# A list scheduler gets other weights: attention with a gated mixture on one Trainium2 core

## The chip, the core and the metric

The kernel runs on one core of a Trainium2 chip. The metric is the device time of one execution in microseconds (us); for the kernel before, three executions took 1042.3, 1046.54 and 1048.9 us, median 1046.54. TensorE (PE) multiplies matrices into PSUM, VectorE (DVE), ScalarE (ACT) and GpSimd (POOL) work on tiles, and SyncE (SP) issues all the transfers here: loads, stores, and transfers that transpose on the way.

## The reference

```python
kv_pool = kv.reshape(B, H // r, r, W // r, r, C).mean(axis=(2, 4))    # r = 4
k = v = kv_pool.reshape(B, -1, C) @ w_sr                              # 768 keys of 128
s = scale * (q @ k.transpose(0, 2, 1)); s = s - s.max(-1, keepdims=True)
a = np.exp(s); a /= a.sum(-1, keepdims=True) + 1e-09
x = a @ v
gate_pre[t] = sum over the five taps k of conv_w[k] * x[t - 4 + k]
out = (1 / (1 + np.exp(-gate_pre)) * (x @ w_val)) @ w_out
```

There are 4 batches of 12288 queries of 128 channels. All is float32, and the kernel keeps that accuracy by splitting values into a high and a low part.

## The kernel before

The queries are cut into groups of 512 columns, 24 to a batch, counted here from 0 to 95 and on (the last 512 columns make two half groups), and each group into four row blocks of 128, counted 0 to 3. For each row block PE makes one score block (L480: high query by high key, high by low, low by high, six matmuls into a PSUM tile `s` of 128 x 768), VectorE takes the row maximum (`nm`, L492), ScalarE the exponential with the row sum (L499), VectorE the reciprocal (`r`, L508 and L513), ScalarE writes the high half of the normalised row as fp16 (`hl`, L527), and VectorE the low half (`hl`, L538, called `lo` below). That last one is the last reader of the score tile. There are three such tiles, so a score waits until the `lo` of the score three places ahead of it is done.

Two row blocks at a time go from `hl` to `pt` by a transposing transfer (L551), two transfers to a group: the first for row blocks 0 and 1, the second for 2 and 3. When both are there, PE adds up 18 attention-value products (L622) into `av`; ScalarE copies that to `x` (L640); GpSimd makes five taps and four sums of the gate (L679, L687); ScalarE takes its tanh (L698); PE makes the value product (L702), VectorE multiplies (`h`, L706), PE makes the output product (L711, into the one PSUM tile `m`, as L702 does), ScalarE copies it out (`o`, L716), and every second group a store goes (L739).

The keys and values of a batch are made ahead, while the batch before is worked on: 16 loads (`kvt`, L279), each summed by VectorE in two parts (`pool`, L291), then projections (L314, L400). Queries are loaded for two groups at a time (L452).

Each engine executes its instructions in the order in which the program issues them. That order is made before anything runs, by a list scheduler (the class `Plan`). Every step is entered with its engine, a duration, a due time (a shift from the table `DUE`, measured from the group's time `t0`, the group's number times `PERIOD`), the steps it waits for and the buffers that it takes and gives back. `order()` then goes through a model of time: of the engine whose next step can begin first, it takes, of the steps that can begin within `WAIT` of it, the one with the earliest due time; on SP, a copy that follows a copy has its due time lowered by `CLUMP`. A step's result is there after its duration and a lag, a transfer's after a lead, its duration and a tail. Nothing of this model is in the program that runs; only the order is. Transfers of both kinds are issued on the one SP queue, in order. In the model the second transposition of a group also waits for the first one's end, since the first takes the `pt` tile (`owner`); the transfers write different halves of it.

Of the kernel before, what the change touches and what calls it, by code (L numbers as in the profile page):

```python
# [19 lines left out]
PIECES = 16  # L20
PARTS = 2

PERIOD = 10.09
DUE = dict(keys=-40.9, vals=-34.18, q=-55.15, qh=8.39, ql=-72.29,
           score=(-7.32, -5.54, -6.8, -6.2), max=(-13.84, -0.53, 9.94, -17.87),
           exp=(2.41, -23.38, 0.25, -11.15), hi=(-29.46, -24.26, -5.96, -31.79),
           lo=(12.82, -20.44, -2.27, 2.53), turn=(1.5, 15.54, 23.77, 4.89), pe=7.53, thi=54.02,
           tlo=9.93, r=(-44.99, -41.46, -38.33, -16.57), grid=-1.44, av=20.99, avs=4.41,
           halo=59.69, x=42.03, gate=31.71, th=61.17, val=48.0, h=0.01, out=29.31,
           evac=16.32, store=49.62)  # L30


class Step:
# [8 lines left out]
class Plan:  # L42
# [2 lines left out]

    EDGE = 0.04
    LAG = dict(PE=0.16, ACT=0.1, DVE=0.085, POOL=0.04, SP=0.0)
    WAIT = dict(PE=0.14, ACT=0.41, DVE=0.11, POOL=0.05, SP=0.32)
    DMA_LEAD, DMA_TAIL, CLUMP = 1.3, 0.8, 23.19

    def __init__(self):
        self.steps, self.stock = [], {}
# [14 lines left out]
    def order(self):  # L67
        left, later = {}, {}
        ready = {}
        for s in self.steps:  # L70
            left[s] = len(s.after)
            for a in s.after:
                later.setdefault(a, []).append(s)
            if not left[s]:
                ready.setdefault(s.eng, []).append((s.start, s))
        free = {e: 0.0 for e in ("PE", "ACT", "DVE", "POOL", "SP")}
        last = {e: "" for e in free}
        dma = 0.0
        until, placed = {}, []
        while any(ready.values()):  # L80
            best = None
            for e, items in ready.items():
                ests = []
                for at, s in items:
                    t = max(at, free[e])
                    for name in s.takes:
                        stock = self.stock[name]
                        t = max(t, min(stock)[0]) if stock else 1e18
                    if t < 1e17:
                        ests.append((t, s))  # L90
                if not ests:
                    continue
                t0 = min(t for t, _ in ests)
                s = min((s.due - (s.kind == last[e] == "copy") * self.CLUMP, n, s)
                        for n, (t, s) in enumerate(ests) if t <= t0 + self.WAIT[e])[2]
                t0 = next(t for t, x in ests if x is s)
                if best is None or t0 < best[0]:
                    best = (t0, e, s)
            assert best, "no step can begin"
            t, e, s = best  # L100
            ready[e] = [x for x in ready[e] if x[1] is not s]
            for name in s.takes:
                stock = self.stock[name]
                pick = min(stock)
                stock.remove(pick)
                s.slot[name] = pick[1]
            if e == "SP":
                copy = s.kind == "copy"
                free[e] = t + (0.5 if copy else s.dur)
                switch = 1.0 if last[e] == "copy" and not copy else 0.0  # L110
                dma = max(dma + switch, t + self.DMA_LEAD) + s.dur
                s.end = dma + self.DMA_TAIL
            else:
                free[e] = t + s.dur
                s.end = t + s.dur + s.lag
            last[e] = s.kind
            placed.append(s)
            for owner, name in s.frees:
                owner.users[name] -= 1
                until[owner, name] = max(until.get((owner, name), 0.0), s.end)  # L120
                if not owner.users[name]:
                    self.stock[name].append((until[owner, name] + self.EDGE, owner.slot[name]))
            for n in later.get(s, ()):
                left[n] -= 1
                if not left[n]:
                    at = max([n.start] + [a.end + self.EDGE for a in n.after])
                    ready.setdefault(n.eng, []).append((at, n))
        assert len(placed) == len(self.steps), "steps that wait for each other"
        return placed
# [13 lines left out]
def cost(us, n):  # L143

    return 0.06 + (us - 0.06) * n / NT
# [3 lines left out]
def attn_moe_kernel(ctx, tc, qT, kvT, w_sr, w_moe, outT):  # L149
# [12 lines left out]
    HALO = TAPS - 1  # L162
    T = PERIOD
    D = DUE
# [3 lines left out]
    plan = Plan()  # L168
# [267 lines left out]
    def group(g, prev, nxt):  # L436
        st, n, w = g.st, g.n, g.n * P
        t0 = g.at * T
# [6 lines left out]
        ld = g.io.ld  # L445
        if off == 0 or g.i == 1:
            cols = GQ if g.i < 2 else 2 * GQ

            def load():
                if off == 0:  # L450
# [4 lines left out]
            ld = plan.add("SP", 1.6 * cols / (2 * GQ), at, load, [ld],  # L455
                          takes=("q",) if off == 0 else (), start=at)
# [7 lines left out]
        def ql():  # L464
# [1 line left out]
            nc.gpsimd.tensor_tensor(out=g.ql, in0=g.io.q[:, mine], in1=g.qh.bitcast(F32),  # L466
                                    op=ALU.subtract)

        s_qh = plan.add("ACT", cost(0.51, n), t0 + D["qh"], qh, [ld], takes=("qh",))
        s_ql = plan.add("POOL", cost(1.23, n), t0 + D["ql"], ql, [s_qh], takes=("ql",),  # L470
                        frees=[(g.io.ld, "q")])
        g.hls, g.los, g.ready = {}, {}, []
# [46 lines left out]
        def straight(j, sc, r):  # L519
# [4 lines left out]
            def hi():  # L524
                if own:
# [4 lines left out]
                            takes=("hl",) if own else ())  # L530
# [5 lines left out]
            def lo():  # L536
# [1 line left out]
                v.scalar_tensor_tensor(out=hl[:, half, 1], in0=sc.tile[:, :NK], scalar=r.tile,  # L538
                                       in1=hl[:, half, 0], op0=ALU.mult, op1=ALU.subtract)
            s_lo = plan.add("DVE", 0.925, t0 + j * T / 4 + D["lo"][j], lo, [s_hi],  # L540
                            frees=[(sc, "s"), (r, "r")])
            g.los[j] = s_lo
            alone = not half and j + 1 in g.turned
            if not (half or alone):
# [1 line left out]
            width, j0 = (1, j) if alone else (2, j - 1)  # L546

            def turn():
                if g.pt_by is s_t:
# [1 line left out]
                nc.sync.dma_start_transpose(  # L551
                    out=g.pt[:, j0:j0 + width].rearrange("p j k q -> p (j k) q"),
                    in_=g.hls[j // 2][:, :width].rearrange("p j a k -> p (j a k)"))
            s_t = plan.add("SP", 1.4 * width, t0 + j * T / 4 + D["turn"][j], turn,
                           [s_lo] if alone else [s_lo, g.los[j - 1]],
                           takes=() if g.pt_by else ("pt",),
                           frees=[(g.hl_by, "hl")], kind="turn")
# [49 lines left out]
        for j in range(n):  # L607
            sc = score(j)
            mx = row_max(j, sc)
            r = unit_over_z(j, sc, expo(j, sc, mx))  # L610
# [6 lines left out]
        avs = []  # L617
        for i, (name, k, a) in enumerate(AV):
# [5 lines left out]
            frees = [(g.pt_by, "pt")] if i == len(AV) - 1 else []  # L624
# [14 lines left out]
        def x():  # L639
# [6 lines left out]
                          start=t0)  # L646
        g.s_halo = s_halo
        g.s_x = plan.add("ACT", cost(0.49, n), t0 + D["x"], x, [avs[-1], s_halo],
                         frees=[(avs[0], "av")])


        late = t0 + D["gate"]
# [19 lines left out]
        else:  # L672
# [12 lines left out]
            def plus(k, tap, before):  # L685
                def run():
                    nc.gpsimd.tensor_tensor(out=g.gate, in0=g.gate, in1=tap.tile, op=ALU.add)  # L687
                return plan.add("POOL", cost(1.24, n), late, run, [tap, before],
                                frees=[(tap, f"tap{k}")])

            gate = gate_by = pool_tap(0)
# [21 lines left out]
        def evac():  # L713
            if off == 0:
# [5 lines left out]
        s_val = plan.add("PE", 0.215 * n, t0 + D["val"], val, [g.s_x, st["wb_by"]]  # L720
                         + ([] if tail else [s_th]), takes=("m",), frees=held)
        s_h = plan.add("DVE", cost(0.59, n), t0 + D["h"], h, [s_val, s_th], takes=("h",),
                       frees=[(s_val, "m"), (s_th, "th")])
        s_out = plan.add("PE", 0.215 * n, t0 + D["out"], out, [s_h], takes=("m",),
                         frees=[(s_h, "h")])
        s_ev = plan.add("ACT", cost(0.48, n), t0 + D["evac"], evac,
# [69 lines left out]
```

## Time and profile before

| what | value |
|---|---|
| three executions | 1042.3, 1046.54, 1048.9 us |
| the profiled execution | 1041.52 us |
| its span, first to last instruction | 1039.7 us |
| mean granted TensorE clock | 0.993 |
| PE, DVE, ACT, POOL busy | 95%, 91%, 85%, 88% of the span |
| transfers | 227 MB, 218 GB/s |

The profile is of one execution. Busy times of PE are modelled at their ends, since matmuls overlap: a busy PE may still have waited for parts of a microsecond. The chain of waits goes back from the last instruction, at each step to what released it.

### The profile page before, as it was taken

How to read it: one execution, taken by the hardware profiler on the slowest of the kernel's cores; microseconds unless marked ns; L12 is line 12 of the kernel's file. 1: busy time of each engine (PE TensorE's matmuls, PEld its weight loads, DVE VectorE, ACT ScalarE, POOL GpSimd, SP SyncE). 2: the span in 40 equal slices, each digit the busy share in tenths (PEclk: the TensorE clock that was granted, in tenths of full speed). 3: DMA queues.
4: the chain of work that ended last, by engine and by line, in shares of the span. 5: the costliest groups of instructions: out<-in, count | busy, mean ns of one | idle time of the engine just before them, and what ended most of it. 6: DMA issues, size and time to landing. Idle time of an engine off the chain costs nothing.

```text
span 1039.7 us, 15330 instructions
## 1 busy us (share of the span) xinstructions
PE 989.9 (95%) x4514; PEld 599.2 (58%) x4514; DVE 941.8 (91%) x1830; ACT 878.7 (85%) x1567; POOL 919.8 (88%) x1047
## 2 busy tenths in 40 slices
PE   1699999999999999999999999999999999999997
PEld 0455555556665555556665555555656666665653
DVE  6889999989899999899989999999998898988985
ACT  1678888889888888789898888888989999999883
POOL 1159989989999999889999999999999999999994
PEclk9899999999999999999999999999999999999999
DMA  8599999999999999999999999999999999999982
GB/s 315 131 200 233 240 244 231 247 233 197 195 241 243 233 242 245 231 234 198 208 219 243 238 237 245 228 251 230 193 202 225 209 199 221 204 209 198 184 177 83
DMA packets 616707, 227.06 MB, mean 218 GB/s; under 512 B 595504, under 2 KB 595888, under 8 KB 616624
## 3 DMA queue, kind: packets, MB, share of 16 engines
q1 hardware_dynamic: 616624, 226.07, 100.3%
q8 instruction: 37, 0.61, 0.2%
q14 instruction: 46, 0.38, 0.1%
HBM read 50.66 MB, written 25.17 MB: 73 GB/s over the span
## 4 chain that ended last, share of the span: by engine, by line
PE 79%; DVE 11%; DMA 7%; ACT 1%; issue 1%; SPq 0%; ACTq 0%; DVEq 0%
PE s L480 33%; PE av L622 30%; PE m L711 8%; PE m L702 7%; DMA pt<-hl 5%; DVE hl L538 4%; DVE nm L492 4%; DMA kvt<-in_kv 2%; DVE pool L291 2%; DVE h L706 1%; ACT hl L527 1%; DVE r L513 0%; PE m L314 0%; DVE wb L375 0%; PE s L314 0%
## 5 line engine op out<-in xcount | busy, mean ns | idle before, releaser
L687 POOL TENSOR_TENSOR gate<-gate,tap 128x512 f32<-128x512 f32 x376 | 481.6, 1281 | 9.8
L538 DVE SCALAR_TENSOR_TENSOR hl<-s,r,hl 128x768 f16<-128x768 f32 x382 | 386.8, 1013 | 49.1 <-ACT hl L527 48.7
L622 PE MATMUL av<-pt,vh 128*128 128x512 f16 (+1 forms) x1164 | 377.9, 379 | 5.0 <-DMA pt<-hl 4.9
L499 ACT ACTIVATE s<-s,nm 128x768 f32<-128x768 f32 x384 | 336.4, 876 | 43.7 <-DVE nm L492 43.1
L527 ACT ACTIVATE hl<-s,r 128x768 f16<-128x768 f32 x382 | 339.0, 906 | 39.1 <-DVE r L513 21.9
L492 DVE TENSOR_REDUCE nm<-s 128x1 f32<-128x768 f32 x384 | 362.7, 945 | 8.7 <-PE s L480 8.0
L480 PE MATMUL s<-kh,qh 128*128 128x512 f32 (+1 forms) x768 | 267.9, 430 | 13.5 <-DVE hl L538 7.7
L679 POOL TENSOR_SCALAR tap<-x,wb 128x512 f32<-128x512 f32 x376 | 253.5, 693 | 0.0
L622 PE MATMUL av<-pt,vl 128*128 128x512 f16 (+1 forms) x582 | 219.7, 378 | 0.0
L480 PEld LDWEIGHTS s<-kh,qh 128*128 128x128 f32 x768 | 133.8, 191 | 132.4 <-issue 59.2
L480 PE MATMUL s<-kl,qh 128*128 128x512 f32 (+1 forms) x768 | 199.1, 341 | 0.0
L480 PE MATMUL s<-kh,ql 128*128 128x512 f32 (+1 forms) x768 | 198.0, 339 | 0.0
L622 PEld LDWEIGHTS <-vh 128*128 128x128 f16 x1164 | 108.5, 98 | 153.1 <-issue 60.8
L466 POOL TENSOR_TENSOR ql<-q,qh 128x512 fp32r<-128x512 f32 (+1 forms) x97 | 122.6, 1264 | 48.8 <-ACT qh L462 48.2
L480 PEld LDWEIGHTS s<-kl,qh 128*128 128x128 f32 x768 | 119.2, 191 | 17.6 <-DVE kl L348 0.5
L480 PEld LDWEIGHTS s<-kh,ql 128*128 128x128 f32 x768 | 119.0, 190 | 17.2
L711 PE MATMUL m<-h,wm 128*128 128x512 f32 (+1 forms) x194 | 102.5, 610 | 2.0 <-DVE h L706 1.9
L702 PE MATMUL m<-x,wb 128*128 128x512 f32 (+1 forms) x194 | 98.5, 589 | 1.2 <-ACT o L716 1.2
L622 PEld LDWEIGHTS <-vl 128*128 128x128 f16 x582 | 57.2, 98 | 66.5 <-issue 23.4
L679 POOL TENSOR_SCALAR gate<-x,wb 128x512 f32<-128x512 f32 x94 | 65.1, 693 | 33.7 <-ACT x L640 26.6
L716 ACT ACTIVATE o<-m 128x512 f32<-128x512 f32 (+1 forms) x97 | 57.6, 593 | 37.9 <-PE m L711 36.7
L513 DVE RECIPROCAL r<-r 128x1 f32<-128x1 f32 x384 | 62.9, 164 | 13.1
(56 smaller groups left out, 592.2 us busy)
## 6 DMA issues: line engine op xcount, KB each, us to landing
kvt<-in_kv SPq DMA_DIRECT2D x64, 384.0 KB, 4.2
q<-in_q SPq DMA_DIRECT2D x47, 512.0 KB, 4.4
out<-o SPq DMA_DIRECT2D x47, 512.0 KB, 3.9
pt<-hl SPq DMA_TRANSPOSE x191, 6.0
q<-in_q SPq DMA_DIRECT2D x2, 256.0 KB, 5.6
raw<-in_w_moe SPq DMA_DIRECT2D x1, 261.0 KB, 5.3
out<-o SPq DMA_DIRECT2D x1, 256.0 KB, 2.0
out<-o SPq DMA_DIRECT2D x2, 128.0 KB, 1.7
```

The costliest lines, as they stand in the source:

```text
L466: nc.gpsimd.tensor_tensor(out=g.ql, in0=g.io.q[:, mine], in1=g.qh.bitcast(F32), op=ALU.subtract)
L480: nc.tensor.matmul(t[:, c0:c1], a[:, sl], k[:, c0:c1], start=(i == 0), stop=(i == 2))
L492: v.tensor_reduce(out=s.tile, in_=sc.tile[:, :NK], axis=AX.X, op=ALU.max, negate=True)
L499: nc.scalar.activation(out=sc.tile[:, :NK], in_=sc.tile[:, :NK], func=AF.Exp, bias=mx.tile, accum_out=sc.tile[:, NK:NK + 1])
L513: v.reciprocal(out=s.tile, in_=e.tile)
L527: nc.scalar.activation(out=g.hls[j // 2][:, half, 0], in_=sc.tile[:, :NK], func=AF.Copy, scale=r.tile)
L538: v.scalar_tensor_tensor(out=hl[:, half, 1], in0=sc.tile[:, :NK], scalar=r.tile, in1=hl[:, half, 0], op0=ALU.mult, op1=ALU.subtract)
L622: nc.tensor.matmul(g.av, st[name][:, k * P:(k + 1) * P], g.pt[:, :, a * NCH + k], start=(i == 0), stop=(i == len(AV) - 1))
L679: nc.gpsimd.tensor_scalar(out=s.tile, in0=src(k), scalar1=wt(k), scalar2=1.0, op0=ALU.mult, op1=ALU.mult)
L687: nc.gpsimd.tensor_tensor(out=g.gate, in0=g.gate, in1=tap.tile, op=ALU.add)
L702: nc.tensor.matmul(g.m, st["wb"][:, :C], g.x[:, HALO:], start=True, stop=True)
L711: nc.tensor.matmul(g.m2, wout, g.h, start=True, stop=True)
```

## The change

`PERIOD`, all of `DUE`, `WAIT` and the transfer figures of the model get other numbers; some durations and lags of single steps too; and the model's SP queue is held longer by a transposition (until `TURN_TAIL` before its end, or 1.05 of its duration, whichever is later, where it was its duration). The steps, their buffers and what they wait for stay.

```diff
-PERIOD = 10.09
-DUE = dict(keys=-40.9, vals=-34.18, q=-55.15, qh=8.39, ql=-72.29,
-           score=(-7.32, -5.54, -6.8, -6.2), max=(-13.84, -0.53, 9.94, -17.87),
...
+PERIOD = 10.07
+DUE = dict(keys=-51.54, vals=-33.1, q=-59.95, qh=11.92, ql=-52.61,
+           score=(-9.11, -6.7, -6.23, -7.04), max=(-11.45, 1.22, 7.36, -15.65),
...
-    WAIT = dict(PE=0.14, ACT=0.41, DVE=0.11, POOL=0.05, SP=0.32)
-    DMA_LEAD, DMA_TAIL, CLUMP = 1.3, 0.8, 23.19
+    WAIT = dict(PE=0.13, ACT=0.31, DVE=0.12, POOL=0.01, SP=0.7)
+    DMA_LEAD, DMA_TAIL, TURN_TAIL, CLUMP = 1.5, 0.9, 1.7, 25.3
...
-                free[e] = t + (0.5 if copy else s.dur)
                 switch = 1.0 if last[e] == "copy" and not copy else 0.0
                 dma = max(dma + switch, t + self.DMA_LEAD) + s.dur
                 s.end = dma + self.DMA_TAIL
+                free[e] = t + 0.5 if copy else max(t + 1.05 * s.dur, s.end - self.TURN_TAIL)
...
-            s_t = plan.add("SP", 1.4 * width, t0 + j * T / 4 + D["turn"][j], turn,
+            s_t = plan.add("SP", 1.45 * width, t0 + j * T / 4 + D["turn"][j], turn,
```

What the order becomes is shown at three places, all around groups 27 to 32, where the keys of batch 2 are loaded during batch 1. The first is the SP queue. Names are buffer and tile number; two rows with the same `pt` are the two transpositions of one group. Before, from the first transposition of group 28 to the second of group 29:

```order
L551 DMA_TRANSPOSE pt0_3677<-hl0_3584 128x24x128
L279 DMA kvt0_3725<-in_kv 128x768
L279 DMA kvt1_3737<-in_kv 128x768
L551 DMA_TRANSPOSE pt0_3677<-hl1_3661 128x24x128
L551 DMA_TRANSPOSE pt1_3785<-hl2_3735 128x24x128
L452 DMA q1_3813<-in_q 128x1024
L739 DMA out_0<-o0_3746 128x1024
L551 DMA_TRANSPOSE pt1_3785<-hl3_3787 128x24x128
```

After, from the first transposition of group 27 (`pt3_3574`) to the second of group 29:

```order
L551 DMA_TRANSPOSE pt3_3574<-hl1_3472 128x24x128
L551 DMA_TRANSPOSE pt0_3687<-hl0_3598 128x24x128
L551 DMA_TRANSPOSE pt3_3574<-hl3_3549 128x24x128
L551 DMA_TRANSPOSE pt0_3687<-hl2_3667 128x24x128
L551 DMA_TRANSPOSE pt1_3807<-hl1_3734 128x24x128
L279 DMA kvt2_3844<-in_kv 128x768
L279 DMA kvt3_3855<-in_kv 128x768
L452 DMA q1_3861<-in_q 128x1024
L739 DMA out_0<-o0_3729 128x1024
L551 DMA_TRANSPOSE pt1_3807<-hl0_3785 128x24x128
```

The four copies of two groups now stand in one run instead of two, and the first transposition of group 28 stands ahead of the second of group 27. Over the whole program such a pair of groups comes 14 times in the new order and never in the old. In the stretches without loads a copy stood behind the two transpositions of a group, and now stands between them.

The second place is PE, between score 1 of group 29 and score 0 of group 30, which takes its buffer. Before, the first rows behind score 1 of group 29 (six more attention products and score 3 follow ahead of score 0 of group 30):

```order
L702 MATMUL m0_3701<-x0_2831,wb1_2823 128x512
L480 MATMUL s2_3707<-kh1_2631,qh2_3436 128x512
L480 MATMUL s2_3707<-kh1_2631,qh2_3436 128x256
L480 MATMUL s2_3707<-kl1_2652,qh2_3436 128x512
L480 MATMUL s2_3707<-kl1_2652,qh2_3436 128x256
L480 MATMUL s2_3707<-kh1_2631,ql2_3450 128x512
L480 MATMUL s2_3707<-kh1_2631,ql2_3450 128x256
L622 LDWEIGHTS vh1_2787
L622 MATMUL av0_3721<-pt3_3541,vh1_2787 128x512
L711 MATMUL m0_3727<-h0_3716,wm_69 128x512
L622 LDWEIGHTS vl1_2802
L622 MATMUL av0_3721<-pt3_3541,vl1_2802 128x512
```

After, from behind score 1 of group 29 (the rest of score 3 and then at once score 0 of group 30 follow):

```order
L711 MATMUL m0_3710<-h0_3704,wm_69 128x512
L480 MATMUL s2_3720<-kh1_2251,qh2_3409 128x512
L480 MATMUL s2_3720<-kh1_2251,qh2_3409 128x256
L480 MATMUL s2_3720<-kl1_2265,qh2_3409 128x512
L480 MATMUL s2_3720<-kl1_2265,qh2_3409 128x256
L480 MATMUL s2_3720<-kh1_2251,ql2_3434 128x512
L480 MATMUL s2_3720<-kh1_2251,ql2_3434 128x256
L702 MATMUL m0_3737<-x2_3522,wb1_2705 128x512
L711 MATMUL m0_3753<-h1_3746,wm_69 128x512
L480 MATMUL s0_3765<-kh1_2251,qh2_3409 128x512
L480 MATMUL s0_3765<-kh1_2251,qh2_3409 128x256
L480 MATMUL s0_3765<-kl1_2265,qh2_3409 128x512
```

The attention products of group 27 have moved behind score 0 of group 30, all 18 in one run, and an L711 stands directly behind its own L702. In the whole program PE changes 241 times from attention products to a score before, and 233 times after.

The third place is VectorE, where a load's sum (`pool`) stands. Before, the first load behind the first transposition of group 30 (`kvt2_3977`) is summed behind the maximum of score 3 of group 31 (`nm1_4031`):

```order
L538 SCALAR_TENSOR_TENSOR hl2_3983<-s2_3916,r9_3975,hl2_3983 128x768
L538 SCALAR_TENSOR_TENSOR hl2_3983<-s0_3937,r0_3996,hl2_3983 128x768
L508 SCALAR_TENSOR_TENSOR r11_4017<-s1_3955,unit_61 128x1
L513 RECIPROCAL r2_4028<-r11_4017 128x1
L492 TENSOR_REDUCE nm1_4031<-s2_4009 128x1
L291 TENSOR_REDUCE pool0_3300<-kvt2_3977 128x24
```

After, the first load behind the first transposition of group 29 (`kvt2_3844`) is summed behind the maximum of score 3 of group 30 (`nm3_3891`):

```order
L492 TENSOR_REDUCE nm3_3891<-s1_3871 128x1
L508 SCALAR_TENSOR_TENSOR r4_3899<-s0_3846,unit_61 128x1
L513 RECIPROCAL r6_3902<-r4_3899 128x1
L291 TENSOR_REDUCE pool0_3054<-kvt2_3844 128x24
L538 SCALAR_TENSOR_TENSOR hl3_3829<-s2_3833,r3_3889,hl3_3829 128x768
L538 SCALAR_TENSOR_TENSOR hl2_3906<-s0_3846,r6_3902,hl2_3906 128x768
```

In both, one group lies between the transposition ahead of the load and the sum; in the new order that transposition itself stands behind four others in a row.

## Rows read from the trace of the kernel before

**Rows 1.** The page: busy time of each engine (share of the span), and the transfers' rate in 40 slices of the span.

```profile
PE 989.9 (95%) x4514; PEld 599.2 (58%) x4514; DVE 941.8 (91%) x1830; ACT 878.7 (85%) x1567; POOL 919.8 (88%) x1047
...
GB/s 315 131 200 233 240 244 231 247 233 197 195 241 243 233 242 245 231 234 198 208 219 243 238 237 245 228 251 230 193 202 225 209 199 221 204 209 198 184 177 83
```

**Rows 2.** Busy time by stretch, four stretches cut where the batches turn over: stretch, its length, then busy us (and instructions) of PE, PE's weight loads, DVE, ACT and POOL, granted clock, share and rate of the transfers. The last stretch, and the sum of all four.

```profile
756.20:1005.90 249.70, 249.63 (x1153) 152.40 (x1152) 222.78 (x426) 223.63 (x398) 240.08 (x272) 1.00 0.99 205
sum 925.40, PE 915.39 PEld 554.17 DVE 855.37 ACT 818.60 POOL 876.67; mean PE 228.85 PEld 138.54 DVE 213.84 ACT 204.65 POOL 219.17
```

**Rows 3.** The chain of waits between 300 and 345 us, two groups of a stretch with loads: start, length, what.

```profile
319.37 0.86 PE m L702 x2
320.23 1.05 PE s L480 x6
...
325.11 2.61 PE av L622 x12
...
339.60 0.86 PE m L702 x2
```

**Rows 4.** The timeline between 900 and 925 us, a stretch without loads: start, length, engine, line and operation. The end of a score, the value product of one group and of the next, the score that takes the buffer, and the first attention product of a group.

```profile
905.53 0.51 PE L480 MATMUL s<-kh,ql 128*128 128x512 f32 x2
...
905.87 1.02 PE L702 MATMUL m<-x,wb 128*128 128x512 f32 x2
...
911.49 0.59 PE L480 MATMUL s<-kh,qh 128*128 128x512 f32 x2
...
915.85 1.02 PE L702 MATMUL m<-x,wb 128*128 128x512 f32 x2
...
918.68 0.38 PE L622 MATMUL av<-pt,vh 128*128 128x512 f16 x1
```

**Rows 5.** The timeline of the SP queue between 326 and 350 us (loads): start, how long the issue holds the queue, what.

```profile
323.25 8.49 SPq L551 DMA_TRANSPOSE pt<-hl  x2
331.79 1.05 SPq L279 DMA_DIRECT2D kvt<-in_kv  x2
332.94 8.90 SPq L551 DMA_TRANSPOSE pt<-hl  x2
341.93 0.53 SPq L452 DMA_DIRECT2D q<-in_q  x1
343.03 0.34 SPq L739 DMA_DIRECT2D out<-o  x1
343.47 8.78 SPq L551 DMA_TRANSPOSE pt<-hl  x2
```

**Rows 6.** The same of the SP queue between 906 and 920 us (no loads).

```profile
906.00 3.59 SPq L551 DMA_TRANSPOSE pt<-hl  x1
909.69 0.53 SPq L452 DMA_DIRECT2D q<-in_q  x1
911.41 8.13 SPq L551 DMA_TRANSPOSE pt<-hl  x2
```

**Rows 7.** The timeline between 329 and 338 us: the way of one score block, from its last matmuls over maximum, high half and low half to the next score in its buffer.

```profile
330.00 0.52 PE L480 MATMUL s<-kh,ql 128*128 128x512 f32 x2
...
330.72 0.95 DVE L492 TENSOR_REDUCE nm<-s 128x1 f32<-128x768 f32 x1
...
334.04 0.89 ACT L527 ACTIVATE hl<-s,r 128x768 f16<-128x768 f32 x1
...
334.97 1.02 DVE L538 SCALAR_TENSOR_TENSOR hl<-s,r,hl 128x768 f16<-128x768 f32 x1 [0.34 <-ACT hl L527]
...
336.13 0.59 PE L480 MATMUL s<-kh,qh 128*128 128x512 f32 x2
```

**Rows 8.** Who waited for whom, PE: us in total, times, longest.

```profile
PE av L622 <- DMA pt<-hl: 4.9, 7, 0.9
```

**Rows 9.** The transpositions (how long an issue holds the queue, in ns, min/median/max), their landing after the issue, one late landing from the chain of waits, and the landing of the loads behind the start.

```profile
L551 SPq DMA_TRANSPOSE pt<-hl x191: 2880/3717/6558, 34.7 to 1011.4; - x191
...
DMA to landing us min/median/max: 4.6/6.0/9.3
...
137.31 9.03 DMA pt<-hl
...
DMA to landing us min/median/max: 3.4/3.9/6.3
```

**Rows 10.** Around 420 us: from the chain of waits the value products ahead and behind and a load; from the timeline VectorE's sum of that load and the next score, with the idle time before each and what ended it in brackets; and the stretch from 424.5 to 427 us with the granted clock (the third figure from the end).

```profile
411.26 0.86 PE m L702 x2
...
414.52 5.87 DMA kvt<-in_kv
...
435.26 0.86 PE m L702 x2
...
420.42 0.55 DVE L291 TENSOR_REDUCE pool<-kvt 128x24 f32<-128x384 f32 x1 [2.31 <-DMA kvt<-in_kv]
...
423.16 0.59 PE L480 MATMUL s<-kh,qh 128*128 128x512 f32 x2 [1.93 <-DVE r L508]
...
424.50:427.00 2.50, 2.50 (x5) 1.37 (x6) 2.50 (x3) 1.43 (x4) 2.00 (x4) 0.50 1.17 239
```

**Rows 11.** The timeline of PE at the end of the program, where an L711 follows its own L702.

```profile
1028.41 1.10 PE L702 MATMUL m<-x,wb 128*128 128x512 f32 x2
1030.37 1.12 PE L711 MATMUL m<-h,wm 128*128 128x512 f32 x2 [0.86 <-DVE h L706]
```

More of the change, by code (lines that the diff above doesn't have):

```diff
@@ L21 @@
 PARTS = 2
-PERIOD = 10.09
-DUE = dict(keys=-40.9, vals=-34.18, q=-55.15, qh=8.39, ql=-72.29,
-           score=(-7.32, -5.54, -6.8, -6.2), max=(-13.84, -0.53, 9.94, -17.87),
[L26 to L30, printed above, removed]
+PERIOD = 10.07
+DUE = dict(keys=-51.54, vals=-33.1, q=-59.95, qh=11.92, ql=-52.61,
+           score=(-9.11, -6.7, -6.23, -7.04), max=(-11.45, 1.22, 7.36, -15.65),
+           exp=(-10.02, -18.03, 5.52, -8.91), hi=(-20.54, -25.94, -10.8, -36.78),
+           lo=(8.83, -56.87, -0.25, -1.79), turn=(24.53, 12.45, 5.45, 5.14), pe=9.87, thi=27.66,
+           tlo=31.15, r=(-39.49, -44.12, -34.32, -11.39), grid=0.16, av=20.26, avs=5.48,
+           halo=77.01, x=41.77, gate=27.88, th=54.09, val=46.93, h=-7.7, out=14.11, evac=-6.98,
+           store=58.22)
 class Step:
@@ L467, in ql @@
                                     op=ALU.subtract)
-        s_qh = plan.add("ACT", cost(0.51, n), t0 + D["qh"], qh, [ld], takes=("qh",))
+        s_qh = plan.add("ACT", cost(0.51, n), t0 + D["qh"], qh, [ld], takes=("qh",), lag=0.145)
         s_ql = plan.add("POOL", cost(1.23, n), t0 + D["ql"], ql, [s_qh], takes=("ql",),
@@ L540, in straight @@
             s_lo = plan.add("DVE", 0.925, t0 + j * T / 4 + D["lo"][j], lo, [s_hi],
-                            frees=[(sc, "s"), (r, "r")])
+                            frees=[(sc, "s"), (r, "r")], lag=0.19)
             g.los[j] = s_lo
@@ L648, in group @@
         g.s_x = plan.add("ACT", cost(0.49, n), t0 + D["x"], x, [avs[-1], s_halo],
-                         frees=[(avs[0], "av")])
+                         frees=[(avs[0], "av")], lag=0.17)
         late = t0 + D["gate"]
@@ L687, in run @@
                     nc.gpsimd.tensor_tensor(out=g.gate, in0=g.gate, in1=tap.tile, op=ALU.add)
-                return plan.add("POOL", cost(1.24, n), late, run, [tap, before],
+                return plan.add("POOL", cost(1.26, n), late, run, [tap, before],
                                 frees=[(tap, f"tap{k}")])
@@ L722, in group @@
         s_h = plan.add("DVE", cost(0.59, n), t0 + D["h"], h, [s_val, s_th], takes=("h",),
-                       frees=[(s_val, "m"), (s_th, "th")])
+                       frees=[(s_val, "m"), (s_th, "th")], lag=0.15)
         s_out = plan.add("PE", 0.215 * n, t0 + D["out"], out, [s_h], takes=("m",),
```

## The prediction, made blind

> **What bounds the kernel now.** I went from the page to the stretches between the batches, then to one period of each kind of stretch, then to the two things that touch there: the SP queue and the score buffers. The page [rows 1] shows TensorE busy for 95% of the span; the other engines follow at 85 to 91%. Cut where the batches turn over [rows 2], TensorE is busy 915 of the 925 us of the body. The last stretch, 756 to 1006 us, has no key/value loads and TensorE busy 249.6 of 249.7 us; there one group takes 9.98 us, from one value product (L702) at 905.87 to the next at 915.85 [rows 4]. Where the next batch's keys are loaded ("load stretch" below), two groups take 20.23 us, from 319.37 to 339.60, against 2 x 9.98 = 19.96 [rows 3].
>
> Two loops explain the difference. In the load stretch the SP queue never rests: from 323.25 to 343.47 us every issue starts within 0.7 us of the end of the one before it, and the round of two loads, one query copy, one store and four transpositions takes 20.2 us, which is the pair's time [rows 5]. In the last stretch the same queue has pauses, as from 910.22 to 911.41 us ahead of a transposition [rows 6]. And TensorE cannot run ahead of the three score buffers: the score block that ends at 330.52 is reduced, exponentiated, normalised and split, its last reader `lo` ends at 335.99, and the score that takes its buffer starts at 336.13, so 5.61 us after the first one ended [rows 7]. In the last stretch the same loop closes in 5.45 us (906.04 to 911.49) [rows 4]. TensorE is the chain, with these two loops close behind it.
>
> **The change, part by part.** No instruction is added or taken away; only order changes. So each part is a place where something comes nearer to, or farther from, what it waits for. I count PE work with rows 3: score block 1.05 us, attention-value product 2.61/12 = 0.22, L702 or L711 0.86.
>
> *Stretches without loads* (groups 70 to 93, and the ends of the other batches): PE's order differs only in two attention products of group g-2 ahead of score 3 of group g instead of three; the buffer loop that closes in 5.45 us contains the same work. A copy now stands between the two transpositions of a group. It puts the later one behind 0.5 us of issue, and even the longest landing, 9.3 us [rows 9], is covered: the one issued at 906.00 [rows 6] is first read at 918.68 [rows 4], 12.7 us later. Zero.
>
> *Queue relief in the load stretch.* Before, loads and query/store copies stand apart, two runs of copies per two groups; now all four copies come in one run, sometimes with six transpositions in a row behind it. Two transpositions behind a run of two copies hold the queue 8.5 to 8.9 us [rows 5], 8.1 behind a single copy [rows 6]: the copies are paid for there too, and fewer runs leave fewer such places. If the relief is complete, TensorE's 19.96 us per pair is the next bound: 0.27 us per pair. Behind the start come 48 loads, two to a pair, so 24 pairs, of which the first four are split up: 20 x 0.27 = -5.4 us. At worst there is no relief, 0; at most all 24, -6.5. I take -5.4, since the queue of rows 5 has nothing but back-to-back issues.
>
> *Scores too near their buffer.* Score 0 of group 30 needs the buffer of score 1 of group 29. Before, PE does L702, a score, eight attention products, L711 and a score in between: 0.86 + 1.05 + 8 x 0.22 + 0.86 + 1.05 = 5.6 us, just the loop. Now it does L711, score, L702, L711, score: 3 x 0.86 + 2 x 1.05 = 4.7 us. It waits 0.75 us against 5.45, 0.9 against 5.61. In groups 8 to 69 there are 16 such places under 5.3 us in the new order, and 3 in the old. Added up in order, each wait pushing what follows, they cost 8.0 us now and 1.3 before against a loop of 5.45, and 11.4 and 3.1 against 5.6: +6.7 to +8.4 us. At the low end 0, if they fall into waits that are there anyway. I take +6.7, because the loop of rows 4 is the undisturbed one.
>
> *L711 directly behind its L702* happens four times in the body (before only in the tail). The tail shows its price: L702 starts at 1028.41, L711 at 1030.37, 1.96 - 0.86 = 1.1 us of waiting for `h` [rows 11]. Three of the four stand just ahead of one of the near scores and spend its wait, so +1 us; 0 to 4.4.
>
> *Transpositions out of order.* Fourteen times the first transposition of group g+1 is issued ahead of the second one of g; before, never. SP is in order, so group g's second one waits until g+1's `lo` is done. For g = 27: from the end of score 1 of group 28, 5.45 us to its `lo`, 3.7 us of queue for its transposition, then 4.6, 6.0 or 9.3 us to the landing of the other [rows 9]: 13.8, 15.2 or 18.5. PE's work over the same way is seven scores (7.4), 18 products (3.9) and four L702/L711 (3.4): 14.7, and the near scores' 0.75 on top: 15.4. So no wait at the median, 3.1 us at the worst landing, 14 x 3.1 = 43 us if all were the worst. Waits of this kind cost 4.9 us in the profile [rows 8], one of them behind a landing of 9.0 us after copies [rows 9]. I take 0: as many remain.
>
> *Loads and their sums.* [...] That pair takes 24.0 us, 411.26 to 435.26, so 3.8 more than 20.2 [rows 10]. Whether it stays is open: -3.8 to +23 (ten places, below). I take 0. The start gains or loses some tenths: +0.5 for nearer scores there.
>
> Sum: -5.4 + 6.7 + 1 + 0 + 0 + 0.5 = **+2.8 us**. The profiled execution took 1041.5 us, so 1044.3; the median of the three runs, 1046.5, stands 5.0 above it, so about **1049 us**.
>
> [...] A transposition of 128 x 3072 fp16 values, 786 KB, holds the queue for 3.7 us [rows 9], 212 GB/s, against 315 GB/s in the first slice of the page [rows 1], which is copies alone. [...]
>
> **The rivals.** *First, the queue frees more than it costs* (faster). The relief is complete, the 4.9 us of late transpositions go with it, the stall at 420 us does not return, and the near scores fall into waits that are no longer visible: -5.4 - 4.9 - 3.8 = -14.1, so 1027.4 and with the 5.0 about 1032 us. For it: all of these rows hang on one saturated queue. Against: sixteen near places do not depend on the queue.
>
> *Second, VectorE runs into loads that have not landed* (slower). The loads now follow transposition 0 of a group that has itself three others ahead of it. For the load summed after the row maximum of score 3 in group 30: from the end of score 1 of group 28, 5.45 us to its `lo`, four transpositions at 3.7, 3.9 us to the load's landing [rows 9]: 24.2 us; PE's way to there is 9.0 to score 1 of group 29, 13.3 to score 3 of group 30, 1.1 for the maximum: 23.4. Short by 0.8 before any wait. In the old order the load stands behind one transposition: 5.45 + 3.7 + 3.9 = 13.1 against 15.6. By sums of this kind ten loads of groups 8 to 69 fall short by some 1 to 3 us, and none did. If each costs what VectorE waited at 420 us, 10 x 2.3 = +23: 1041.5 + 2.8 + 23 + 5 = 1072 us; with half of them, 1061. It decides from a shortfall that TensorE's own waits do not cover, about 1 us. For it: VectorE is in order and every score passes through it twice. Against: the waits of the other terms give the loads time.
>
> *Third, the queue is not what sets the load pace.* Then the relief is 0 and the rest stays: 2.8 + 5.4 = +8.2, 1055 us. Were a transposition worth its bytes at 315 GB/s, 2.5 us, the round would be 4 x 2.5 + 1.84 MB/315 GB/s = 15.8 us, under TensorE's 19.96, and the cause of 20.23 would be elsewhere. The back-to-back issues of rows 5 speak against it. [...]
>
> **How the numbers follow.** Forecast 0.48, first rival 0.22, second 0.20, third 0.10. The forecast is the likeliest case, 1049 us; its own range is 1043 to 1056. The range 1032 to 1066 leaves out half of the first rival and the upper half of the second, 2 in 10 together. One per cent, 10.5 us, is about what a measurement of this kernel can tell from no change. Faster than 1036: 0.18 of the first rival and 0.02 of the forecast, 0.20. Slower than 1057: 0.18 of the second, 0.04 of the third, 0.05 of the forecast, 0.27. Within: 0.53.
>
> **What would show it.** Relief: pairs near 19.96 us in the load stretch and pauses in SP's timeline there. Near scores: TensorE waiting for `hl` of VectorE just ahead of L480, at the 16 places, 0.3 to 1.5 us each. Out-of-order transpositions: more or less than 4.9 us of attention products waiting for `pt`. Loads: VectorE's sums (L291) waiting for `kvt`, now 2.3 us in the body. The last stretch has to stay at 9.98 us per group; if it does not, the argument about order is wrong as a whole.

## The result: 0.7% slower

Seven executions of the changed kernel take 1051.83 to 1054.31 us, median 1052.33; seven of the kernel before, beside them, have a median of 1046.54. The ratio is 1.0067, with a 95% interval of 1.0045 to 1.0088: +5.8 us by the medians. The forecast was 1049 us, its own range 1043 to 1056.

The profiled execution took 1054.31 us, 12.8 more than that of before, which stood 5.0 under its median. Its page, as in [rows 1]:

```profile
PE 994.4 (94%) x4514; PEld 598.5 (57%) x4514; DVE 940.7 (89%) x1830; ACT 879.9 (84%) x1567; POOL 918.3 (87%) x1047
```

Where the time went shows in the busy time by stretch, cut at the value products of groups 17, 41, 65 and 90 in both kernels (columns as in [rows 2]). Before, the two stretches with loads behind the start:

```profile
260.00:508.80 248.80, 245.88 (x1123) 148.53 (x1122) 231.73 (x451) 218.25 (x390) 233.90 (x266) 0.99 1.06 229
508.80:756.20 247.40, 244.53 (x1123) 147.34 (x1122) 231.48 (x451) 218.18 (x390) 233.75 (x265) 1.00 1.06 230
```

After, these two and the last:

```profile
259.10:514.50 255.40, 248.16 (x1122) 147.21 (x1121) 231.89 (x451) 219.09 (x391) 233.30 (x264) 0.99 1.05 224
514.50:768.90 254.40, 245.91 (x1122) 147.18 (x1121) 231.70 (x451) 219.13 (x391) 233.39 (x264) 1.00 1.05 223
768.90:1018.30 249.40, 249.40 (x1152) 152.29 (x1151) 222.58 (x423) 224.50 (x400) 240.58 (x273) 1.00 1.00 204
```

The loss is in the stretches with loads, 6.6 and 7.0 us; the start is 0.9 us shorter, and the last stretch keeps its time [rows 2]. That is more than the 5.8 us of the medians. The stretches compare better than whole executions, because the start varies: a kernel below that keeps the order of before (the short sums) took 6.0 us more than before up to group 17, and then the same 248.7 and 247.5 us. Who waited in the whole program, as in [rows 8], for PE and its weight loads:

```profile
PE av L622 <- DMA pt<-hl: 7.1, 7, 2.1
...
PEld L622 <- DMA pt<-hl: 3.8, 4, 2.2
```

10.9 us of waiting for transpositions, where it was 4.9. The SP queue's timeline shows how a transposition comes to be late, around those of groups 34 and 35:

```profile
397.14 3.72 SPq L551 DMA_TRANSPOSE pt<-hl  x1
...
403.77 3.59 SPq L551 DMA_TRANSPOSE pt<-hl  x1
...
407.42 3.71 SPq L551 DMA_TRANSPOSE pt<-hl  x1
```

and VectorE's low halves (`lo`) around them, with the first attention product of group 34:

```profile
397.13 1.01 DVE L538 SCALAR_TENSOR_TENSOR hl<-s,r,hl 128x768 f16<-128x768 f32 x1
...
402.69 1.02 DVE L538 SCALAR_TENSOR_TENSOR hl<-s,r,hl 128x768 f16<-128x768 f32 x1
...
413.10 0.39 PE L622 MATMUL av<-pt,vh 128*128 128x512 f16 x1
```

The `lo` that ends at 398.14 is the last that group 34's second transposition needs, and the queue is free at 400.86. But the first of group 35 stands ahead, and its `lo` ends at 403.71. So the queue stands still for 2.91 us, then takes that one, and group 34's goes out at 407.42, 6.6 us after it could have. It lands at 413.06, and the product starts 0.04 us later, so it had no slack left; at groups 30 and 48 the products wait 1.91 and 2.06 us. There are eight such pauses of 0.9 to 3.9 us ahead of an out-of-order pair in the two stretches, 16.1 us together. All the queue's pauses over 0.3 us came to 8.5 and 10.6 us before (270 to 500 and 520 to 745 us), and come to 16.6 and 15.8 after.

### The profile page after: what moved, and what is told of

It is laid out like the page before. It is cut to its first block, busy times and chain, and to the rows that moved or that the text cites. A ratio compares the mean times of both kernels' runs of the same rounds, so it can differ in the third digit from the quotient of the medians.

```text
span 1052.5 us, 15285 instructions
## 1 busy us (share of the span) xinstructions
PE 994.4 (94%) x4514; PEld 598.5 (57%) x4514; DVE 940.7 (89%) x1830; ACT 879.9 (84%) x1567; POOL 918.3 (87%) x1047
## 5 line engine op out<-in xcount | busy, mean ns | idle before, releaser
L538 DVE SCALAR_TENSOR_TENSOR hl<-s,r,hl 128x768 f16<-128x768 f32 x382 | 385.3, 1013 | 45.0 <-ACT hl L527 43.2
L622 PE MATMUL av<-pt,vh 128*128 128x512 f16 (+1 forms) x1164 | 367.5, 380 | 7.1 <-DMA pt<-hl 7.1
L480 PE MATMUL s<-kh,qh 128*128 128x512 f32 (+1 forms) x768 | 262.1, 423 | 15.5 <-DVE hl L538 8.5
L622 PE MATMUL av<-pt,vl 128*128 128x512 f16 (+1 forms) x582 | 220.5, 379 | 0.0
L480 PEld LDWEIGHTS s<-kh,qh 128*128 128x128 f32 x768 | 133.0, 191 | 133.4 <-issue 57.4
L480 PE MATMUL s<-kl,qh 128*128 128x512 f32 (+1 forms) x768 | 198.6, 340 | 0.0
L480 PE MATMUL s<-kh,ql 128*128 128x512 f32 (+1 forms) x768 | 198.1, 339 | 0.0
L622 PEld LDWEIGHTS <-vh 128*128 128x128 f16 x1164 | 106.7, 98 | 145.0 <-issue 49.3
L480 PEld LDWEIGHTS s<-kl,qh 128*128 128x128 f32 x768 | 119.0, 190 | 17.9 <-DVE kl L348 0.5
L480 PEld LDWEIGHTS s<-kh,ql 128*128 128x128 f32 x768 | 118.7, 190 | 17.0
L711 PE MATMUL m<-h,wm 128*128 128x512 f32 (+1 forms) x194 | 103.1, 613 | 5.5 <-DVE h L706 5.1
L622 PEld LDWEIGHTS <-vl 128*128 128x128 f16 x582 | 57.2, 98 | 76.9 <-issue 27.3
L702 PE MATMUL m<-x,wb 128*128 128x512 f32 (+1 forms) x194 | 98.5, 589 | 1.2 <-ACT o L716 1.2
L706 DVE SCALAR_TENSOR_TENSOR h<-th,m 128x512 f32<-128x512 f32 (+1 forms) x97 | 65.4, 674 | 10.4 <-PE m L702 10.0
```

The source lines that it names most:

```text
L480: nc.tensor.matmul(t[:, c0:c1], a[:, sl], k[:, c0:c1], start=(i == 0), stop=(i == 2))
L622: nc.tensor.matmul(g.av, st[name][:, k * P:(k + 1) * P], g.pt[:, :, a * NCH + k], start=(i == 0), stop=(i == len(AV) - 1))
L702: nc.tensor.matmul(g.m, st["wb"][:, :C], g.x[:, HALO:], start=True, stop=True)
L706: v.scalar_tensor_tensor(out=g.h, in0=g.th, scalar=1.0, in1=g.m, op0=ALU.add, op1=ALU.mult)
L711: nc.tensor.matmul(g.m2, wout, g.h, start=True, stop=True)
```

## The experiments

Theory Q says that these pauses make the loss. Theory N is my prediction's: the scores too near their buffer. To change one thing at a time, most kernels let the scheduler make its order, edit the finished list of one engine, and issue the steps by these lists; what isn't edited keeps its place. The times are medians, and the ratios are to the kernel before on the same chip (medians of 1044.0 to 1045.9 us there).

**Transpositions in order.** On the list of SP:

```diff
+def in_order(sp):
+    for i in range(len(sp) - 1):
+        a, b = sp[i].name, sp[i + 1].name
+        if a and b and a[0] == b[0] == "T" and a[1] == b[1] + 1:
+            sp[i], sp[i + 1] = sp[i + 1], sp[i]
```

> The changed kernel with one edit of its finished order: on the SP queue, the 14 transpositions that stand ahead of the second one of the group before change places with it; every other engine keeps its order. Theory Q (the queue's head waits for scores not yet made, while a transposition that is ready stands behind it): the eight pauses of 0.9 to 3.9 us read there in the trace, 16 us of queue time, go, and half of it or more reaches the end: 1041 to 1046 us, against 1052.3 of the changed kernel. Theory N (the scores that stand too near their buffer make the loss, as I predicted): 1051 to 1053.

1045.62 us, ratio 1.0004 (0.9987 to 1.0020): by the times, the loss is gone. The waits of PE and of its weight loads:

```profile
PEld L645 <- DMA pt<-hl: 1.1, 1, 1.1
...
PE av L645 <- DMA pt<-hl: 0.8, 1, 0.8
```

1.9 us instead of 10.9. Group 34's second transposition now goes out as soon as the first has left the queue, the second of these rows:

```profile
396.48 3.16 SPq L573 DMA_TRANSPOSE pt<-hl  x1
...
399.73 3.75 SPq L573 DMA_TRANSPOSE pt<-hl  x1
```

The two stretches with loads:

```profile
260.30:510.90 250.60, 246.15 (x1122) 146.74 (x1122) 231.81 (x450) 218.84 (x391) 233.25 (x264) 1.00 1.08 228
510.90:760.10 249.20, 245.55 (x1122) 146.82 (x1121) 231.52 (x450) 219.04 (x391) 233.30 (x264) 1.00 1.07 228
```

They are 10.0 us shorter than in the changed kernel, where the loss was 13.6; what makes the other 3.6 is open. The near scores are all still there in this kernel. Theory Q holds for most of the loss, and N doesn't explain it.

**The same edit the other way round,** on the kernel before:

```diff
+        if a and b and a[0] == b[0] == "T" and b[1] == a[1] + 1 and a[1] in (
+                5, 7, 9, 12, 25, 27, 30, 34, 38, 48, 52, 54, 56, 60):
+            sp[i], sp[i + 1] = sp[i + 1], sp[i]
```

> The kernel before with one edit of its finished order: at 13 of the 14 groups where the changed kernel does so (at the fourteenth a copy stands between the two), the second transposition of the group and the first of the next change places on the SP queue; nothing else moves. Theory Q: the order of the transpositions is by itself enough for the loss; putting them in order gave the changed kernel 6.5 us back, so this costs 3 to 9 us, a ratio of 1.003 to 1.009 to the kernel before. If it takes the changed kernel's other places too, such as the near scores, to make them cost: ratio 0.999 to 1.002.

1085.44 us, ratio 1.0400 (1.0366 to 1.0434): about 40 us for 13 swaps, 3.1 each, and far more than expected. The waits:

```profile
PE av L646 <- DMA pt<-hl: 34.3, 14, 4.3
...
PEld L646 <- DMA pt<-hl: 18.0, 8, 2.8
```

52.3 us in all. So a swap alone is enough for a loss. In the changed kernel the products stand later, and that hides most of it: by the two traces, the first product of such a group starts 12.7 us after the end of the next group's score 1 in the kernel before, and 15.45 us in the changed kernel with its transpositions in order (medians; more on this way below).

**Scores farther from their buffer.** On PE's list, products from behind are drawn ahead of each near score and between adjoining L702 and L711:

```diff
+        if k == "S" and 8 <= s.name[1] < 70 and len(ends) > 2:
+            need = ends[-3] + loop - at
...
+        while need > 0.0:
...
+            pe.insert(i, pe.pop(j))
```

> The changed kernel with the other edit: on PE, attention products from behind are drawn ahead of each score of groups 8 to 69 that starts less than 5.45 us of PE work after the end of the score whose buffer it takes, and between an L702 and an L711 of the same group; the SP queue keeps its order. Theory N: the 16 near scores and the adjoining L702 and L711 cost 6.7 + 1 us, so 1044 to 1046 us. Theory Q: the places are waits that the late transpositions cause anyway, 1050 to 1052.

1080.68 us, ratio 1.0335 (1.0302 to 1.0367). Both edits together:

> Both edits of the changed kernel together. Theory Q: as with the transpositions in order alone, 1041 to 1046 us. Theory N: as with the scores alone, 1044 to 1046. If both mechanisms are real and separate, and the queue relief that I predicted too: 1046.5 - 5.4 = 1041 or below. If the relief is not real: 1046 to 1048, the time of the kernel before.

1059.64 us, ratio 1.0140 (1.0114 to 1.0166). No theory gave these times. The edit was too coarse: it drew 76 products ahead, some of them to where their transposition hadn't landed (41 us of waits for `pt` in the first, 12 in the second). It says nothing on the near scores' price, so I made a finer one, on top of the transpositions in order: 50 products, for scores under 5.3 us from their buffer only those that follow directly, and up to four steps behind for L711.

```diff
+            if kind(s) == "S" and at < ends[-3] + 5.3:
+                need = ends[-3] + 5.45 - at
+            if kind(s) == "O" and pe[i - 1].name == ("V", s.name[1]):
+                need, far = 1.0, 4
```

> The changed kernel with its transpositions in order, as before, and besides on PE attention products that follow directly drawn ahead of 13 of the 16 near scores, 1 to 6 each, and five between each of two pairs of L702 and L711 in a row; these products are ones that the transpositions in order leave 1 to 7 us of slack in most places. Theory N, my prediction's price: 16 near scores and the pairs cost 6.7 + 1 us, so 1039 to 1040 us against 1045.6 with the transpositions alone in order. If the price was too high (the waits before these scores add up to 2.9 us in the trace, those before L711 to 1.6 us): 1042 to 1044.

1053.81 us, ratio 1.0091 (1.0059 to 1.0122): 8 us slower than with the near scores in place. Two places lose 2.5 and 4.2 us, each to a product drawn ahead of its `pt` (waits of 2.2 and 2.9 us). No other edited place gains more than 0.23 us on its pair of groups, and two lose 0.4 and 1.0. The value products of groups 54 and 60 enclose the near scores 61.3 and 62.0 (score 3 of group 61, score 0 of group 62), of which 62.0 waits 0.34 us. With them near (transpositions in order):

```profile
637.44 1.02 PE L726 MATMUL m<-x,wb 128*128 128x512 f32 x2
...
706.55 1.02 PE L726 MATMUL m<-x,wb 128*128 128x512 f32 x2
```

and moved away:

```profile
644.89 1.02 PE L754 MATMUL m<-x,wb 128*128 128x512 f32 x2
...
713.97 1.02 PE L754 MATMUL m<-x,wb 128*128 128x512 f32 x2
```

69.11 us against 69.08. The price of these two is zero. The longest wait of a near score, 1.1 us at 40.0, lies where the edit lost 2.5 us, so its price isn't separated.

**Copies in one run,** the queue relief alone, on the kernel before:

```diff
+            sp[i:i + 6] = rest + sp[i + 4:i + 6] + two
```

(`two` are the query copy and the store, `rest` the two transpositions behind them, then come the loads.)

> The kernel before with one edit of its finished order: in 14 rounds of the load stretches the query copy and the store move back on the SP queue, behind the two loads of the next round, so that the four copies of a round stand in one run; nothing else moves. It tests the queue relief alone. My prediction: 0.27 us for each of the 14 rounds, -3.8 us, so about 1043 us, with pairs of groups at 19.96 to 20.0 us there instead of 20.23. Without relief (my third rival): 1046.5, pairs at 20.2 us.

1042.82 us, ratio 0.9978 (0.9958 to 0.9998), so 2.3 us faster by the ratio. But its profiled execution has the same span as before, within 0.1 us, its two stretches with loads together are 1.0 us longer (497.2 against 496.2), and the pairs that took 20.23 us still do. From the timeline of PE:

```profile
329.44 1.02 PE L728 MATMUL m<-x,wb 128*128 128x512 f32 x2
...
349.67 1.02 PE L728 MATMUL m<-x,wb 128*128 128x512 f32 x2
```

20.23 us, the time of [rows 3], to the hundredth; and in the same pair the queue has a pause. From its timeline:

```profile
341.23 3.63 SPq L575 DMA_TRANSPOSE pt<-hl  x1
...
346.76 3.02 SPq L575 DMA_TRANSPOSE pt<-hl  x1
349.83 1.05 SPq L302 DMA_DIRECT2D kvt<-in_kv  x2
```

The issue before ends at 344.86, and the next begins 1.90 us later. The copies in one run do free queue time, and the pair doesn't get shorter by it: a full queue was not what made 20.23 us out of 19.96. Nor is every wait for `pt` a loss, for there are more of them here than in the changed kernel:

```profile
PE av L647 <- DMA pt<-hl: 9.2, 10, 1.8
...
PEld L647 <- DMA pt<-hl: 4.8, 6, 1.4
```

**What of a load costs?** Three kernels from before; the first cuts VectorE's sums behind the start to one of 16 values (`few`):

```diff
-                                in_=ld.tile.rearrange("c (k s) -> c k s", s=RR)[:, part * n:][:, :n],
+                                in_=ld.tile.rearrange("c (k s) -> c k s", s=RR)[:, part * n:][:, :n, :few],
```

> The kernel before with the sums of the loads of batches 1 to 3 cut to the first of each 16 values (so the keys and values of these batches are not the reference's); loads, queue and order stay. The copies in one run left the pairs at 20.23 us, so the queue may not be what sets them. Theory V (VectorE's sums, which stand between the steps of the score loop, set the pair's time in the load stretches): pairs fall to 19.9 to 20.0 us and the whole by 24 x 0.27 = 6.5 us or somewhat more, ratio 0.990 to 0.995. Theory of my prediction (the SP queue sets it): pairs stay at 20.2 us, ratio 0.998 to 1.0.

1044.82 us, ratio 0.9990 (0.9970 to 1.0010). A sum takes 0.18 us instead of 0.53, and the pair still 20.24 us:

```profile
316.07 1.02 PE L703 MATMUL m<-x,wb 128*128 128x512 f32 x2
...
336.31 1.02 PE L703 MATMUL m<-x,wb 128*128 128x512 f32 x2
```

Its stretches, in the order of before, from the cuts at groups 17, 41 and 65:

```profile
266.00:514.70 248.70, 244.27 (x1122) 147.50 (x1121) 222.44 (x451) 218.43 (x390) 234.21 (x265) 1.00 1.07 228
514.70:762.20 247.50, 244.68 (x1123) 147.45 (x1122) 222.56 (x451) 218.37 (x390) 234.26 (x266) 1.00 1.07 230
```

The second leaves the loads out behind the start; the sums read a tile that is set once:

```diff
+                if not first:
+                    return
```

> The kernel before without the 48 loads of batches 1 to 3 (their sums read a tile set once, so keys and values of these batches are not the reference's); VectorE's sums and all orders stay. Theory of my prediction: the queue gets 0.5 us of issue and the bytes of 48 loads back, pairs fall to 19.96 us, ratio 0.990 to 0.995. Theory V: pairs stay at 20.2 us and only the waits for late transpositions and the stall at 420 us go, ratio 0.995 to 0.999.

1033.02 us, ratio 0.9890 (0.9862 to 0.9917): 11.5 us by the ratio. Its profiled execution ran at a granted clock of 0.85 throughout and can't be compared, so the pair's time without loads isn't known at full clock. The waits for `pt` [rows 8] and the stall at 420 us [rows 10] make 4.9 + 3.8 = 8.7 us of the 11.5, so this run doesn't tell the theories apart. The third issues the loads from ScalarE:

```diff
-                nc.sync.dma_start(out=t, in_=kvT[b, i])
+                (nc.sync if first else nc.scalar).dma_start(out=t, in_=kvT[b, i])
```

> The kernel before with the 48 loads of batches 1 to 3 issued by ScalarE, each at its place in the program's order, instead of by SyncE; all else stays. Leaving the loads out brought a ratio of 0.989, rearranging the copies on the SP queue left the pairs at 20.23 us. If what costs is the loads' place in the one in-order queue: 0.989 to 0.993, pairs at 19.96 us. If it is the bytes that all transfers share: 0.998 to 1.000, pairs at 20.2 us. If ScalarE's issues stand in the way of its exponentials: 1.002 or more.

1051.13 us, ratio 1.0087 (1.0059 to 1.0115). Products wait more for their transposition than in before's profile (4.9 us):

```profile
PE av L639 <- DMA pt<-hl: 20.4, 16, 3.6
```

But this profiled execution took 1065.62 us, the others 1049.01 to 1058.05. VectorE's waits for the high half grow too, from 48.7 us in before's profile to 59.8. So moving the loads out of the one queue didn't help; whether the loss comes from their issues on ScalarE (the third case) or from the transfers, this run doesn't tell.

**The halves of the change.**

> One half of the change alone: the model's new durations, lags, WAIT, transfer figures and the longer hold of its SP queue, with the old PERIOD and DUE. In the order that comes out, 15 times the first transposition of a group stands ahead of the second one of the group before; 19 scores of groups 8 to 69 are under 5.3 us from their buffer. Theory Q: the order of the transpositions makes the loss, so this half has it: ratio to the kernel before 1.004 to 1.02. If the new weights make it: 0.998 to 1.002.

1057.38 us, ratio 1.0134 (1.0111 to 1.0156), as theory Q has it, but not by its way: products wait only 2.8 us for `pt`, while the scores' waits for `lo` grow from 7.7 us:

```profile
PE s L480 <- DVE hl L538: 14.3, 19, 2.7
```

With 19 near scores in it, this kernel doesn't clear them: here theory N is open.

> The other half alone: the new PERIOD and DUE with the old model. Only one transposition stands ahead of the second one of the group before (at group 7), and 8 scores are under 5.3 us from their buffer. Theory Q: ratio 0.997 to 1.003. If the new weights make the loss: 1.004 to 1.008.

1061.28 us, ratio 1.0169 (1.0150 to 1.0188). Each half alone is slower than both together, and the second against theory Q's number. Its two stretches with loads take 2.1 and 4.4 us more than before's; most of its loss is in the last stretch, 10.38 us per group instead of 9.99:

```profile
764.30:1023.80 259.50, 258.32 (x1153) 150.17 (x1152) 222.72 (x425) 223.69 (x400) 240.72 (x273) 1.00 0.93 197
```

PE waits for no transposition there. So an order made anew can lose elsewhere, and the halves say little of the whole. What makes 10.38 us isn't shown. The median score starts there 0.15 us after the `lo` that frees its buffer, where the kernel before has 0.46 (from the rows of L480 and L538), which points at the score loop.

**The cause behind the order.** In the model the second transposition of a group is ready only when the first has landed, and the next group's first doesn't wait for that, so it can be taken ahead. The changed kernel with this wait alone shortened:

```diff
+            s.begin = t
...
-                    at = max([n.start] + [a.end + self.EDGE for a in n.after])
+                    at = max([n.start] + [(a.begin if a.kind == n.kind == "turn" else a.end) + self.EDGE for a in n.after])
```

> The changed kernel with one edit of its model: the second transposition of a group is ready once the first has begun, no longer once it has ended; all weights stay and the whole order is made anew. In it no transposition stands ahead of the second one of the group before, 15 scores of groups 8 to 69 are still under 5.3 us from their buffer, and two L711 of these groups stand directly behind their L702. Theory Q: the model's false wait is what put the 14 transpositions out of order, so the loss goes: ratio to the kernel before 0.995 to 1.002, products waiting for their transposition under 3 us in all. If the near scores are what costs after all: 1.004 to 1.008. The halves of the change showed that an order made anew can lose elsewhere, so a loss in a stretch without loads would speak for neither.

1043.27 us, ratio 0.9996 (0.9985 to 1.0008). All transpositions are in order and the loss is gone, with 15 scores still near. Products wait 6.7 us for `pt` in the whole program, more than I gave:

```profile
PEld L623 <- DMA pt<-hl: 4.6, 5, 1.4
...
PE av L623 <- DMA pt<-hl: 2.1, 4, 0.8
```

It beats the changed kernel, not the one before. Only the four copies in one run stand a little below that.

## Why the prediction came out close, and where it was wrong

The time was right within 3.3 us, but by errors that cancelled, and that is luck: of the four terms that made the forecast, none is found at its size in the runs, and the one that made the result stood at zero.

*Stretches without loads, zero:* right, 249.40 us against 249.70, and the one transposition behind a copy is covered, as said.

*Queue relief, -5.4:* wrong. The step that failed is the first one, that the saturated queue sets 20.23 us: with the queue given a pause of 1.90 us the pair stays to the hundredth. Sums and copies aside, what is left is the score loop: between 260 and 410 us the median score starts 0.15 us after the `lo` that frees its buffer, in the kernel before, with the copies in one run and with short sums alike (from the timeline's rows of L480 and L538); in the last stretch of the kernel before it is 0.46. I take the loop for the bound, but no run gave the loop a fourth buffer, so this is argued and not shown. At most 2.3 us came, by a ratio whose interval just excludes 1, and none of it shows in the stretches. The third rival thus was right that there is no relief. Its round of 15.8 us had a transposition at 2.5 us, which neither trace shows: in the changed kernel one holds the queue for 3.74 us (median of 191), against 3.72 before [rows 9], so the rival came true by another way.

*Near scores, +6.7:* wrong in size: the loss went with all of them in place, and in the kernel without the false wait with 15 such scores. In the changed kernel five of the 16 wait, 2.9 us together; the example, score 0 of group 30, doesn't. All scores wait 8.5 us for `lo`, 7.7 before, and 5.1 against 4.1 for `r`. A sum that lets every wait push what follows takes PE for the only bound. If the loop paces anyway, a score that starts early waits and one that starts late does not, and the group takes as long; that is argued as above.

*L711 behind L702, +1:* the waits are there (1.6 us of PE for `h` in the two stretches with loads), but the product put between at group 25 waited 0.87 us instead and the pair of groups 24 and 25 kept its time within 0.03 us. No net price was found.

*Out-of-order transpositions, 0, ends -4.9 and +43:* this is the term that made the result. It measured +6.7 us (1052.3 to 1045.6) and, in before's order, about +40. The step that failed is that the sum for group 27, worked out at the median landing, was taken for all 14 places. As a median it holds. From the end of score 1 of the next group to the landing it says 15.2 us, and the changed kernel takes 15.7; to the first product it says 15.4, and with the transpositions in order that takes 15.45 (medians of the 14 places, from the rows of L480, L551 and L622 and their like in the two traces). But the one goes from 14.3 to 16.9 and the other from 14.6 to 16.4, and only the late ones cost: groups 30, 48, 54 and 56 fall short by 2.0, 2.1, 1.0 and 1.4 us, three others by 0.4 or less and seven, group 27 among them, by nothing, 7.0 in all. At group 30 that score ends at 352.08 in the changed kernel, and at 353.21 with the transpositions in order (second pair of rows; the product is group 30's first):

```profile
351.57 0.51 PE L480 MATMUL s<-kh,ql 128*128 128x512 f32 x2
...
368.91 0.61 PE L622 MATMUL av<-pt,vh 128*128 128x512 f16 x1 [1.91 <-DMA pt<-hl]
```

```profile
352.70 0.51 PE L501 MATMUL s<-kh,ql 128*128 128x512 f32 x2
...
367.95 0.39 PE L645 MATMUL av<-pt,vh 128*128 128x512 f16 x1
```

16.8 us against 14.7. And from 368.9 to 372.3 us, right after that wait, the granted clock is 0.50. In before's order the products come 12.7 us after that score (10.8 to 13.5), so there every swap falls short: the landings of the swapped kernel come 14.8 us after it (median), and the shortfalls add up to 35 us over the 13. That this made 3.1 us each, the figure of my worst landing, is luck.

*Loads and sums, 0:* the second rival didn't come: behind the start VectorE's only waits for a load are 0.77 us, at 423, and 0.76, at 700. So the stall at 420 us (2.31 us [rows 10]) didn't return at its size; whether its 3.8 us came back, no run separates.

Of the signs that I named, the waits for `pt` led to the cause; the pauses of SP, which I had named as the sign of relief, were the sign of the loss.

## What to carry to other kernels

In an in-order queue near saturation, look at what stands at its head: an entry that is not ready holds up everything behind it (2.91 us ahead of group 35's first transposition, with group 34's ready), and the price depends on how much slack the consumers have there (0.5 us a place in one order, 3.1 in the other). Where a sum says "no wait at the median", work it out place by place: waits don't average out against slack. A wait that costs nothing in the place where it shows (a score ahead of its buffer) can be told from one that does only by moving it and comparing the time between two fixed points. When a planner's figures are set to measurements, first see that its waits are those of the machine: here taking out one false wait took the loss away, though no gain over the kernel before was left.

## What I had not expected

Between the two kernels with transpositions in order, near scores in place and moved away, the pairs of groups away from an edited place agree to 0.05 us, so that such edits show their price place by place. And moving 48 loads to another engine's queue didn't help: the longest landing of a transposition between 270 and 500 us was 13.4 us there, against 9.2 before, so the transfers may share more than the queue. That is a guess from one long execution.
